# Pooled attention, ELU MoE, SoLU MoE: one pooling moved in the opening, the first pair's PSUM banks and the place of later splits changed in the second MoE

## The chip, the cores and the metric

One core of one Trainium2 chip runs the whole program. The metric is the device time of one execution in microseconds (us), lower is better.

## What is computed

Three stages follow each other on 4608 tokens of 512 features, all in float32:

```
# attention: 8 batches, 8 heads, 576 tokens, head_dim 64, keys and values pooled by 8
k_p = k.reshape(B, H, Sp, 8, D).mean(axis=3);  v_p likewise          # Sp = 72
scores = scale * q @ k_p.T;  attn = softmax(scores);  x = attn @ v_p  # heads joined: (4608, 512)
# first MoE, d_ff 2048
h = x @ w_in;  g = where(h > 0, h, exp(min(h, 0)) - 1);  x = g @ w_out
# second MoE, d_ff 1024
h = x @ w_in2;  solu = h * softmax(h)
ln = (solu - mean(solu)) / sqrt(var(solu) + 1e-6) * g_ln;  out = ln @ w_out2
```

The weights come as 64-bit floats and are turned into 32-bit ones on the chip, by integer operations on their two halves.

## The kernel before, in words

**Precision.** An operand of a large product is split into a high part (a rounded copy, made on ScalarE) and a low part (the difference, made on VectorE or GpSimd); a product is then three matmuls: high by high, low by high, high by low. `xh`, `xl` are the parts of the tokens, `wh`, `wl` of the first weights, `woh`, `wol` of the second, `gh`, `gl_` of the activations.

**Attention.** A unit is one batch and one pair of heads, 32 units in all (`NP` = 4 to a batch). `att_setup(i)` (L122) pools a unit's keys by a reduction on VectorE (L139) and copies the result into a block-diagonal tile; it pools the values on GpSimd (`pool_tree`, L118) for units 0 to 3, and by a reduction on VectorE (L148) for the others. Scores go to PSUM, `att_max` (L176) and `att_exp` take the exponential on ScalarE, `att_soft` (L198) normalises: sum L203, L204, reciprocal L205, product L207. `att_T` transposes on TensorE (L219), `att_V` multiplies by the values, `att_x` (L246) writes `xh` and `xl`.

**The opening.** `startup()` (L689) runs units 0 to 3 and the first weights' conversion (`conv`, L336; `conv_split`, L358) in an order written out by hand, under `tc.manual_schedule()`. All loads are issued from SyncE's queue: keys and queries of units 0 to 3, then values and the first weights (`raw`, L333 for the second weight matrix), then the loads of units 4 and 5 and those after. The keys of all units from 4 on share one buffer (tag `k`, `bufs=1`), so the next load waits until the pooling before has read it. Behind the opening stands `att_setup(NP)` (L773), which is unit 4. Outside of the hand-written part, a scheduling layer sets the order of each engine's instructions, and it may move an instruction ahead of what the code has before it. `with tc.issue_after(x)` puts the block's instructions behind instruction `x` in that order. `gate["soft0"]` is unit 3's L207.

**First MoE.** Nine blocks of 512 tokens by 16 slices of 128 of d_ff. `m_h1` makes 12 matmuls (L461), then comes the ELU (L471 to L492, with `gh` at L485), and `m_o1` makes 12 matmuls (L504) into two PSUM tiles of two banks each, tag A. During block 0 the rest of the weights is converted (L349 to L355) and split (L369, L370); the attention of the following units goes on beside the blocks. `m_out` copies the sums out (L514 on ScalarE, L516 on VectorE) and stores them.

**Second MoE.** 36 tiles of 128 tokens make 18 pairs. `p2_split(n)` (L532) makes the sums and differences of pair n's tokens and their parts (L540 to L550). The two-by-two product of a pair is seven products (`prod`, L558) of six matmuls each (L565), accumulated in three PSUM banks X, Y, Z: in `p2_h_one` B11 to X, B21 to Y, T1 to Z, T2 to X, in `p2_h_two` T3 to X, in `p2_h_three` T4 to X and B22 to Z. Between products into X, ScalarE copies X out (`snap`, L573), and VectorE adds copies to Y and Z (L585, L594, L603), which gives the two rows of sums `ha` and `hb`. `p2_soft` (L609) has a reduction for the maximum (L613), the exponential on ScalarE (L614), the steps to `e` on VectorE (L617 to L621) and the variance (L623 to L625). `p2_T` transposes `e` on TensorE (L635, tag B) and splits it (`dhl`, L638 on ScalarE); `p2_o` makes 24 matmuls (L650, tag C) and stores the result. The eight PSUM banks are split into tag A (2 tiles of two banks), B (2 of one) and C (2 of one). X and Y are the two halves of one tile of tag A; Z is half of the other.

Of the kernel before, what the change touches and what calls it, by code (L numbers as in the profile page):

```python
# [8 lines left out]
F32 = mybir.dt.float32  # L9
# [4 lines left out]
ALU = mybir.AluOpType  # L14
# [4 lines left out]
def kernel(  # L19
# [15 lines left out]
    nc = tc.nc  # L35
# [86 lines left out]
    def att_setup(i, what="kv"):  # L122
        b, p = units[i]
        early = i < NP
        if early:
            k_t, _, v_t = st["kq", p]
            if "kz" not in st:
                kz = sb.tile([P, 4, 512], F32, name="kz", tag="w", bufs=8)
                nc.vector.memset(kz[:, :, 0:2 * SK], 0.0)
                st["kz"] = kz  # L130
            kp = st["kz"][:, p, 0:2 * SK]
            vt = st["kz"][0:SK, p, 2 * SK:2 * SK + P]
        else:
            k_t, v_t = st.pop(("ld", i))
            kp = kpbd[i % 2]
            vt = p1.tile([SK, P], F32, name=f"vt{i}", tag="vt")
        if "k" in what:
            kr = p1.tile([P, SK], F32, name=f"kr{i}", tag="kr", bufs=1)
            nc.vector.tensor_reduce(kr, k_t.rearrange("p (s t) -> p s t", t=POOL), axis=AX, op=ALU.add)  # L139
            cpy = nc.vector.tensor_copy if early else nc.scalar.copy  # L140
            cpy(kp[0:64, 0:SK], kr[0:64, :])
            cpy(kp[64:128, SK:2 * SK], kr[64:128, :])
        if "v" in what:
            vr = p1.tile([SK, P], F32, name=f"vr{i}", tag="vr", bufs=1)
            if early:
                pool_tree(vr, v_t)
            else:
                nc.vector.tensor_reduce(vr, v_t, axis=AX, op=ALU.add)  # L148
            nc.scalar.mul(vt, vr, 1.0 / POOL)
        st["kp", b, p] = (kp, vt)  # L150
# [381 lines left out]
    def p2_split(n):  # L532

        c, q = divmod(n, 2)
        t = wraw["x", c]
        ta, tb = slice(q * P, (q + 1) * P), slice(256 + q * P, 256 + (q + 1) * P)
        sm = sb.tile([P, 4, 2, P], F32, name=f"xs{n}", tag="cv", bufs=2)
        hi, lo = (xtile(f"x{k}{n}").rearrange("p a f -> p (a f)") for k in "hl")
        tt = nc.vector.tensor_tensor
        tt(sm[:, 0], t[:, 0:2, tb], t[:, 2:4, tb], op=ALU.add)  # L540
        tt(sm[:, 1], sm[:, 0], t[:, 0:2, ta], op=ALU.subtract)
        tt(sm[:, 2], t[:, 0:2, ta], t[:, 0:2, tb], op=ALU.subtract)
        tt(sm[:, 3], t[:, 2:4, ta], sm[:, 1], op=ALU.subtract)
        for src, d in ((t[:, :, ta], slice(0, 512)), (t[:, 2:4, tb], slice(512, 768))):
            h, l = (z[:, d].rearrange("p (k t) -> p k t", t=P) for z in (hi, lo))
            nc.scalar.copy(h, src)
            tt(l, src, h.bitcast(F32), op=ALU.subtract)
        src = sm.rearrange("p s k t -> p (s k t)")
        nc.scalar.copy(hi[:, 768:1792], src)
        tt(lo[:, 768:1792], src, hi[:, 768:1792].bitcast(F32), op=ALU.subtract)  # L550
        xc[n] = (hi, lo)
        if q == 1:
            wraw.pop(("x", c))
# [20 lines left out]
        return t  # L574

    def p2_h_one(n):
        xy = ps.tile([P, 2, 512], F32, name="xy", tag="A")
        z = ps.tile([P, 2, 512], F32, name="z", tag="A")
        X, Y, Z = xy[:, 0], xy[:, 1], z[:, 0]
        ha = p2.tile([P, 2, 512], F32, name="ha", tag="h", bufs=3)  # L580
        hb = p2.tile([P, 2, 512], F32, name="hb", tag="h", bufs=3)
        prod(n, X, "A11", "B11", True, False)
        p1s = snap(X)
        prod(n, Y, "A12", "B21", True, True)
        nc.vector.tensor_tensor(ha[:, 0], Y, p1s, op=ALU.add)  # L585
        prod(n, Z, "S1", "T1", True, False)
        prod(n, X, "S2", "T2", False, False)
        acc[n] = (X, Z, ha, hb, snap(X))
# [20 lines left out]
    def p2_soft(i, h):  # L609
        hv = h.rearrange("p a f -> p (a f)")  # L610
        sc = p2.tile([P, 8], F32, name="sc", tag="sc", bufs=6)
        e = p2.tile([P, DFF2], F32, name="e2", tag="e2", bufs=3)
        nc.vector.tensor_reduce(sc[:, 0:1], hv, axis=AX, op=ALU.max, negate=True)  # L613
        nc.scalar.activation(e, hv, AF.Exp, bias=sc[:, 0:1], accum_out=sc[:, 1:2])  # L614
        nc.vector.tensor_scalar(sc[:, 1:2], sc[:, 1:2], 1e-9, None, op0=ALU.add)
        nc.vector.reciprocal(sc[:, 1:2], sc[:, 1:2])
        nc.vector.scalar_tensor_tensor(  # L617
            e, e, sc[:, 1:2], hv, op0=ALU.mult, op1=ALU.mult, accum_out=sc[:, 2:3]
        )
        nc.vector.tensor_scalar(sc[:, 2:3], sc[:, 2:3], 1.0 / DFF2, None, op0=ALU.mult)  # L620
        nc.vector.tensor_scalar(e, e, sc[:, 2:3], None, op0=ALU.subtract)  # L621

        nc.scalar.activation(hv, e, AF.Square, accum_out=sc[:, 3:4])  # L623
        nc.vector.tensor_scalar(sc[:, 3:4], sc[:, 3:4], 1.0 / DFF2, 1e-6, op0=ALU.mult, op1=ALU.add)
        nc.gpsimd.tensor_tensor(sc[:, 4:5], sc[:, 3:4], mhalf, op=ALU.pow)  # L625
        dts[i] = (e, sc)

    def p2_T(i):
        e, sc = dts[i]
        dhl = p2.tile([P, 2, NC2, P], F32R, name="dhl", tag="dhl", bufs=2)  # L630
        dh, dl = dhl[:, 0], dhl[:, 1]
        for g in range(2):
            pt = ps.tile([P, 512], F32, name="pt2", tag="B")
            for c in range(4):
                nc.tensor.transpose(pt[:, c * P:(c + 1) * P], e[:, (4 * g + c) * P:(4 * g + c + 1) * P], ident)  # L635
            d = slice(4 * g, 4 * g + 4)
            dhv = dh[:, d, :].rearrange("p a t -> p (a t)")
            nc.scalar.copy(dhv, pt)  # L638
            nc.vector.tensor_tensor(
                dl[:, d, :].rearrange("p a t -> p (a t)"), pt, dhv.bitcast(F32), op=ALU.subtract  # L640
            )
        dts[i] = (dh, dl, sc)
# [127 lines left out]
    while nload[0] < NP + 2:  # L770
        att_load(nload[0])
        nload[0] += 1
    att_setup(NP)  # L773

    slots = [(j, f) for j in range(NBLK) for f in range(NF)]
    for si, (j, f) in enumerate(slots):
# [64 lines left out]
    def tiles_of(n):  # L841

        c, q = divmod(n, 2)
        return 4 * c + q + 2, 4 * c + q

    for n in range(NPAIR):
        p2_h_one(n)
        if n == 0:
            p2_h_two(n)
            p2_h_three(n)  # L850
            p2_load(1)
            continue
        a, b = tiles_of(n - 1)
        p2_T(a)
        if n % 2 == 0 and n // 2 + 1 < NT // 512:
            p2_load(n // 2 + 1)
        if n >= 2:
            p2_o(tiles_of(n - 2)[1])
        p2_h_two(n)
        if n + 1 < NPAIR:  # L860
            p2_o(a)
        else:
            p2_T(b)
        p2_h_three(n)
        if n + 1 < NPAIR:
            p2_split(n + 1)
            p2_T(b)

    p2_o(a)
# [41 lines left out]
```

## Time and profile before

| | |
|---|---|
| median of 3 timed runs | 1394.13 us (1390.72 to 1394.84) |
| the profiled execution's own time | 1395.61 us |
| its span | 1393.8 us, 16740 instructions |
| TensorE (PE) matmul busy | 1341.8 us (96% of the span) |
| VectorE (DVE) busy | 844.5 us (61%) |
| ScalarE (ACT) busy | 657.1 us (47%) |
| GpSimd (POOL) busy | 306.0 us (22%) |
| chain that ended last, by engine | PE 87%, DVE 6%, DMA 3%, ACT 2% |

Busy time is the time in which an engine had an instruction under way; a busy TensorE need not run at its full clock. PEld is TensorE's loading of weights, which overlaps with PE. SP is SyncE, whose queue (SPq) issues the loads and stores. The chain is followed back from the last instruction, at each step to what released it. The share of an engine over the whole span is a mean of stages with different limits, so the rows further below are read by stage. "L139" is line 139 of the kernel.

### The profile page before, as it was taken

How to read it: one execution, taken by the hardware profiler on the slowest of the kernel's cores; microseconds unless marked ns; L12 is line 12 of the kernel's file. 1: busy time of each engine (PE TensorE's matmuls, PEld its weight loads, DVE VectorE, ACT ScalarE, POOL GpSimd, SP SyncE). 2: the span in 40 equal slices, each digit the busy share in tenths (PEclk: the TensorE clock that was granted, in tenths of full speed). 3: DMA queues.
4: the chain of work that ended last, by engine and by line, in shares of the span. 5: the costliest groups of instructions: out<-in, count | busy, mean ns of one | idle time of the engine just before them, and what ended most of it. 6: DMA issues, size and time to landing. Idle time of an engine off the chain costs nothing.

```text
span 1393.8 us, 16740 instructions
## 1 busy us (share of the span) xinstructions
PE 1341.8 (96%) x6260; PEld 1072.6 (77%) x6260; DVE 844.5 (61%) x1454; ACT 657.1 (47%) x1273; POOL 306.0 (22%) x245
## 2 busy tenths in 40 slices
PE   2889999999999999999999999999899999999998
PEld 2567778788788788788787778887688888888887
DVE  4898766566566566555554375553675666657463
ACT  1677654444444344444444343433455544555453
POOL 2365322222322223222222222221000000000000
PEclk7699999999999999999999999999999999999999
DMA  9255222122022022111010042444211011101000
GB/s 264 71 178 190 78 95 66 33 95 73 27 95 73 28 93 73 35 57 42 27 39 1 17 165 91 151 181 163 86 48 58 24 53 54 54 23 54 29 18 38
DMA packets 48336, 105.93 MB, mean 76 GB/s; under 512 B 4608, under 2 KB 12800, under 8 KB 46848
## 3 DMA queue, kind: packets, MB, share of 16 engines
q1 hardware_dynamic: 48256, 104.88, 22.5%
q8 instruction: 49, 0.80, 0.2%
q14 instruction: 31, 0.25, 0.1%
HBM read 74.45 MB, written 30.41 MB: 75 GB/s over the span
## 4 chain that ended last, share of the span: by engine, by line
PE 87%; DVE 6%; DMA 3%; ACT 2%; issue 1%; SPq 1%; POOL 0%; POOLq 0%; DVEq 0%; ACTq 0%
PE h L461 26%; PE o L504 26%; PE po L650 13%; PE xy L565 9%; PE z L565 3%; PE at L243 2%; PE pt L635 2%; PE at L164 2%; PE pt L219 2%; DMA raw<-in_w 2%; DMA k<-in_k 1%; ACT es L184 1%; DVE cv L353 0%; PE pr L224 0%; DVE cv L355 0%
## 5 line engine op out<-in xcount | busy, mean ns | idle before, releaser
L444 POOL TENSOR_TENSOR wol<-wo,woh 128x512 fp32r<-128x512 f32 x144 | 202.6, 1407 | 524.5 <-ACT woh L443 524.5
L461 PE MATMUL h<-xh,wh 128*128 128x512 f32 x576 | 237.5, 412 | 0.0
L504 PE MATMUL o<-gh,woh 128*128 128x512 f32 x576 | 227.2, 395 | 2.1 <-ACT gh L485 1.6
L461 PE MATMUL h<-xl,wh 128*128 128x512 f32 x576 | 227.7, 395 | 0.0
L504 PE MATMUL o<-gh,wol 128*128 128x512 f32 x576 | 226.5, 393 | 1.0 <-POOL wol L444 1.0
L461 PE MATMUL h<-xh,wl 128*128 128x512 f32 x576 | 226.4, 393 | 0.4 <-POOL wl L370 0.4
L650 PE MATMUL po<-o,dhl 128*128 128x512 f32 x864 | 208.4, 394 | 0.4 <-ACT dhl L638 0.4
L650 PEld LDWEIGHTS po<-o,dhl 128*128 128x128 f32 x864 | 160.9, 188 | 34.7 <-ACT dhl L638 0.7
L482 DVE TENSOR_SCALAR e<-e 128x512 f32<-128x512 f32 x128 | 54.8, 428 | 217.1 <-ACT e L471 216.7
L471 ACT ACTIVATE e<-h 128x512 f32<-128x512 f32 x128 | 76.3, 596 | 198.5 <-PE h L461 198.5
L485 ACT CAST gh<-e 128x512 fp32r<-128x512 f32 x144 | 89.5, 622 | 151.7 <-DVE e L483 141.6
L461 PEld LDWEIGHTS h<-xh,wh 128*128 128x128 f32 x576 | 109.1, 189 | 33.4 <-issue 13.6
L504 PEld LDWEIGHTS o<-gh,woh 128*128 128x128 f32 x576 | 108.4, 188 | 27.8 <-ACT gh L485 3.4
L461 PEld LDWEIGHTS h<-xl,wh 128*128 128x128 f32 x576 | 108.8, 189 | 25.1
L504 PEld LDWEIGHTS o<-gh,wol 128*128 128x128 f32 x576 | 108.5, 188 | 25.1 <-POOL wol L444 1.9
L461 PEld LDWEIGHTS h<-xh,wl 128*128 128x128 f32 x576 | 109.3, 190 | 21.4 <-POOL wl L370 0.9
L625 POOL TENSOR_TENSOR sc<-sc,mhalf 128x1 f32<-128x1 f32 x36 | 22.0, 611 | 385.4 <-DVE sc L620 346.3
L443 ACT CAST woh<-wo 128x512 fp32r<-128x512 f32 x144 | 89.5, 621 | 35.1 <-PE o L504 33.8
L483 DVE TENSOR_TENSOR e<-e,h 128x512 f32<-128x512 f32 x128 | 88.0, 687 | 3.4
L613 DVE TENSOR_REDUCE sc<-hb 128x1 f32<-128x1024 f32 x18 | 22.0, 1220 | 102.3 <-ACT hb L599 101.7
L565 PE MATMUL xy<-T,xh 128*128 128x512 f32 x216 | 77.1, 398 | 3.9 <-DVE sc L620 2.1
L653 ACT ACTIVATE ot<-po,sc 128x512 f32<-128x512 f32 x36 | 24.7, 687 | 106.6 <-PE po L650 88.4
(565 smaller groups left out, 2253.4 us busy)
## 6 DMA issues: line engine op xcount, KB each, us to landing
raw<-in_w SPq DMA_DIRECT2D x48, 512.0 KB
v<-in_v SPq DMA_DIRECT2D x32, 288.0 KB
x1d<-x1s SPq DMA_DIRECT2D x9, 1024.0 KB
x1r<-x1d SPq DMA_DIRECT2D x9, 1024.0 KB
out<-ot SPq DMA_DIRECT2D x36, 256.0 KB
k<-in_k SPq DMA_DIRECT2D x28, 288.0 KB
q<-in_q SPq DMA_DIRECT2D x28, 288.0 KB
w2d<-cv SPq DMA_DIRECT2D x14, 512.0 KB
```

Source lines behind the costliest of these rows:

```text
L164: nc.tensor.matmul(s[:, t * 2 * SK:(t + 1) * 2 * SK], q_t[:, o:o + P], kp, start=True, stop=True)
L219: nc.tensor.transpose(pt[0:SK, t * P:(t + 1) * P], es[:, 2 * t + h, :], ident)
L443: nc.scalar.copy(oh, t[:, f % 4, :])
L444: nc.gpsimd.tensor_tensor(ol, t[:, f % 4, :], oh.bitcast(F32), op=ALU.subtract)
L461: nc.tensor.matmul(h[:, 0:n], a[g][:, kk, fo:fo + P], x[j][:, kk, 0:n], start=(i == 0), stop=(i == 3 * KDM - 1))
L471: nc.scalar.activation(e[:, 0:n], h[:, 0:n], AF.Exp)
L482: nc.vector.tensor_scalar(e[:, 0:n], e[:, 0:n], 1.0, 1.0, op0=ALU.min, op1=ALU.subtract)
L483: nc.vector.tensor_tensor(e[:, 0:n], e[:, 0:n], h[:, 0:n], op=ALU.max)
L485: nc.scalar.copy(gh[:, 0:n], e[:, 0:n])
L504: nc.tensor.matmul(acc, a[:, dm * P:(dm + 1) * P], x[:, 0:n], start=(f == 0 and m == 0), stop=(f == NF - 1 and m == 2))
L565: nc.tensor.matmul(bank, x[:, o:o + P], w[:, y + k, :], start=(start and m == 0), stop=(stop and m == 5), skip_group_check=True,)
L650: nc.tensor.matmul(po, a[:, c, :], w[c // 4][:, c % 4, :], start=(m == 0), stop=(m == 3 * NC2 - 1))
```

## The change

Three edits. The setup of unit 4 is put behind unit 3's normalisation. The first pair of the second MoE takes three single banks from the tags B, B and C in place of two tiles of tag A. The split of pair n+1 (for n from 1) is put behind the last subtraction (L621) of the second softmax that was written before, the one of pair n-1.

```diff
     def p2_h_one(n):
-        xy = ps.tile([P, 2, 512], F32, name="xy", tag="A")
-        z = ps.tile([P, 2, 512], F32, name="z", tag="A")
-        X, Y, Z = xy[:, 0], xy[:, 1], z[:, 0]
+        if n == 0:
+            X, Y, Z = (ps.tile([P, 512], F32, name="xyz", tag=t) for t in "BBC")
+        else:
+            xy = ps.tile([P, 2, 512], F32, name="xy", tag="A")
+            z = ps.tile([P, 2, 512], F32, name="z", tag="A")
+            X, Y, Z = xy[:, 0], xy[:, 1], z[:, 0]
...
-        nc.vector.tensor_scalar(e, e, sc[:, 2:3], None, op0=ALU.subtract)
+        gate["p2"] = nc.vector.tensor_scalar(e, e, sc[:, 2:3], None, op0=ALU.subtract).ins
...
-    att_setup(NP)
+    with tc.issue_after(gate["soft0"]):
+        att_setup(NP)
...
         a, b = tiles_of(n - 1)
+        before = gate["p2"]
         p2_T(a)
...
         if n + 1 < NPAIR:
-            p2_split(n + 1)
+            with tc.issue_after(before):
+                p2_split(n + 1)
             p2_T(b)
```

In the changed file the lines from L577 on have numbers higher by four, those from L778 on by more.

**The opening on VectorE.** In the order of before, the pooling of unit 4's keys (`kr_367` from `k_354`) stands inside unit 0's softmax (`sm_175`, `es_131`), behind its sum:

```order
 L142 COPY kz<-kr_171 64x72
 L203 TENSOR_REDUCE sm_175<-es_131 128x10
-L139 TENSOR_REDUCE kr_367<-k_354 128x72
 L204 TENSOR_SCALAR sm_175<-sm_175 128x10
 L205 RECIPROCAL sm_175<-sm_175 128x10
```

It has left that place. The poolings of units 5 and 6 (`kr_550`, `kr_748`), which stood a few rows further on inside the same opening, have left it too, and stand in the first block of the first MoE now. Unit 4's stands here, behind unit 3's normalisation (`es_209`) and among the first conversions (`cv`):

```order
 L207 TENSOR_TENSOR es_209<-es_209,sm_286 128x720
 L353 SCALAR_TENSOR_TENSOR cv<-raw,cv 128x1024
-L351 TENSOR_SCALAR cv<-cv 128x1024
+L139 TENSOR_REDUCE kr_367<-k_354 128x72
 L355 SCALAR_TENSOR_TENSOR cv<-raw,cv 128x1024
 L257 TENSOR_TENSOR xl_256<-at_291,xh_255 128x512
+L148 TENSOR_REDUCE vr_371<-v_355 72x128
```

The second conversion's first step (L351) went back behind it.

**The passage between the MoEs on TensorE.** `B_7341` is B11, `T_7509` T2, `T_7511` T3; `xh_7707` and `xl_7708` are the parts of pair 0, `xh_7831` those of pair 1, and `o_8_0`, `o_8_1` are the sums of the last block of the first MoE. The last slice of that block:

```order
 L504 MATMUL o_8_1_7230<-gh,wol 128x512
 L504 MATMUL o_8_1_7230<-gl__7775,woh 128x512
+L565 MATMUL xyz<-B_7341,xh_7707 128x512
+L565 MATMUL xyz<-B_7341,xl_7708 128x512
+L565 MATMUL xyz<-B_7341,xh_7707 128x512 x2
+L565 MATMUL xyz<-B_7341,xl_7708 128x512
 L504 MATMUL o_8_0_7229<-gh,woh 128x512
 L504 MATMUL o_8_0_7229<-gh,wol 128x512
 L504 MATMUL o_8_1_7230<-gh,woh 128x512
```

Five of the six matmuls of the first product of the second MoE have come ahead of the last slice's. In the changed order, farther on, between the products T2 and T3 of pair 0:

```order
L565 MATMUL xyz<-T_7509,xh_7707 128x512
L565 MATMUL xy<-B_7341,xh_7831 128x512
L565 MATMUL xy<-B_7341,xl_7832 128x512
L565 MATMUL xy<-B_7341,xh_7831 128x512 x2
L565 MATMUL xyz<-T_7511,xh_7707 128x512
```

Four matmuls of pair 1 stand there now, where before T3's followed T2's at once; four more stand between T3 and T4.

**A later pair on ScalarE.** `e_8760` and `e_8779` are the results of the two exponentials of one pair, `sn` the copy of X in the pair after it, `xh_8972` and `xh_9151` parts made by the splits of two pairs farther on. Before:

```order
L638 CAST dhl<-pt_8804 128x512
L638 CAST dhl<-pt_8811 128x512
L573 COPY sn<-xy 128x512
L614 ACTIVATE e_8779,sc<-ha,sc 128x1024
L549 CAST xh_8972<-xs_8971 128x1024
L546 CAST xh_9151<-x1r_8866 128x512
L546 CAST xh_9151<-x1r_8866 128x256
L623 ACTIVATE hb,sc<-e_8760 128x1024
```

and after (the names' numbers are one higher, the lines four):

```order
L642 CAST dhl<-pt_8805 128x512
L642 CAST dhl<-pt_8812 128x512
L618 ACTIVATE e_8780,sc<-ha,sc 128x1024
L573 COPY sn<-xy 128x512
L627 ACTIVATE hb,sc<-e_8761 128x1024
```

The copy of X stands behind the second exponential, and the casts of the splits, which stood ahead of the squares (L623, now L627), come later.

## Rows read from the trace of the kernel before

**Rows 1.** Stretches: us, length; busy PE, PEld, DVE, ACT, POOL; clock, DMA share, GB/s.

```profile
0.00:58.00 58.00, 25.89 (x113) 17.14 (x114) 35.24 (x62) 19.28 (x41) 14.50 (x24) 0.66 0.66 193
58.00:157.00 99.00, 90.16 (x398) 68.68 (x399) 88.63 (x105) 71.01 (x187) 54.03 (x32) 0.94 0.47 153
157.00:970.00 813.00, 811.46 (x3828) 650.79 (x3827) 463.46 (x759) 353.72 (x672) 215.49 (x155) 1.00 0.22 72
970.00:1005.00 35.00, 29.74 (x120) 22.29 (x119) 20.49 (x43) 13.30 (x23) 1.68 (x2) 0.95 0.38 145
1005.00:1394.00 389.00, 384.57 (x1805) 313.71 (x1803) 236.66 (x488) 199.79 (x352) 20.32 (x34) 1.00 0.11 41
```

**Rows 2.** Waits of VectorE, 0 to 60 us: total us, waits, longest us.

```profile
DVE kr L139 <- DMA k<-in_k: 13.4, 2, 12.7
```

**Rows 3.** Timeline, 0 to 45 us: start, us, what, [idle time before <- releaser].

```profile
12.40 0.20 DVE L142 COPY kz<-kr 64x72 f32<-64x72 f32 x1
...
15.78 1.95 POOL L118 TENSOR_TENSOR v<-v 72x512 f32<-72x512 f32 x2
15.89 1.22 DVE L142 COPY kz<-kr 64x72 f32<-64x72 f32 x1
16.34 4.75 SPq L333 DMA_DIRECT2D raw<-in_w  x2
17.13 0.90 DVE L203 TENSOR_REDUCE sm<-es 128x10 f32<-128x720 f32 x1
...
30.72 0.75 DVE L139 TENSOR_REDUCE kr<-k 128x72 f32<-128x576 f32 x1 [12.68 <-DMA k<-in_k]
...
32.89 1.89 PE L219 MATMUL pt<-ident,es 128*72 128x128 f32 x8 [18.73 <-DVE es L207]
```

**Rows 4.** Timeline, 44 to 75 us: second conversion on ScalarE, TensorE's first `h`.

```profile
46.27 1.12 ACT L349 ACTIVATE wo<-raw 128x1024 f32<-128x1024 f32 x1
...
57.75 0.80 PE L461 MATMUL h<-xh,wh 128*128 128x512 f32 x1
```

**Rows 5.** Timeline of TensorE, 955 to 992 us.

```profile
971.73 0.50 PE L504 MATMUL o<-gh,woh 128*128 128x512 f32 x1 [0.86 <-ACT gh L485]
...
975.24 0.50 PE L565 MATMUL xy<-B,xh 128*128 128x512 f32 x1 [0.50 <-DVE x1s L516]
...
980.13 0.50 PE L565 MATMUL xy<-T,xh 128*128 128x512 f32 x1 [0.42 <-DVE ha L585]
...
982.46 0.50 PE L565 MATMUL xy<-T,xh 128*128 128x512 f32 x1 [0.68 <-ACT sn L573]
...
986.28 0.39 PE L565 MATMUL z<-B,xh 128*128 128x512 f32 x1
```

**Rows 6.** Timeline of TensorE, 990 to 1030 us: the longest idle time.

```profile
994.16 0.51 PE L565 MATMUL xy<-T,xh 128*128 128x512 f32 x1 [2.14 <-DVE sc L620]
```

**Rows 7.** Timeline of VectorE, 950 to 1000 us: splits beside pair 0's softmax.

```profile
988.83 0.68 DVE L547 TENSOR_TENSOR xl<-x1r,xh 128x512 fp32r<-128x512 f32 x1
...
991.03 1.21 DVE L550 TENSOR_TENSOR xl<-xs,xh 128x1024 fp32r<-128x1024 f32 x1
...
994.47 0.75 DVE L621 TENSOR_SCALAR e<-e,sc 128x1024 f32<-128x1024 f32 x1
```

**Rows 8.** Timeline of TensorE, 1094 to 1112 us, in a later pair.

```profile
1101.41 0.39 PE L565 MATMUL z<-T,xl 128*128 128x512 f32 x1
1101.80 0.50 PE L565 MATMUL xy<-B,xh 128*128 128x512 f32 x1
1102.14 0.39 PE L565 MATMUL xy<-B,xl 128*128 128x512 f32 x1
1102.37 0.62 PE L565 MATMUL xy<-B,xh 128*128 128x512 f32 x2
```

**Rows 9.** Timeline of ScalarE, 1085 to 1112 us, in the same pair.

```profile
1101.15 0.60 ACT L573 COPY sn<-xy 128x512 f32<-128x512 f32 x1
1101.63 1.17 ACT L614 ACTIVATE e<-ha,sc 128x1024 f32<-128x1024 f32 x1
```

## The prediction

> **What bounds the kernel now.** I read the busy time by stretches first, then the waits of the opening, then the timelines of the places that the change touches. [rows 1] cut the span into five stretches. From 157 to 970 us TensorE is busy for 811.46 of 813 us, and from 1005 us on for 384.57 of 389: there it is the bound, and nothing that this change does to other engines can shorten its work. What it loses lies in three places: the first 58 us (busy 25.89, and at a mean granted clock of 0.66, so mostly at the lower of its two levels), the first block of the first MoE from 58 to 157 us (8.84 us idle, clock 0.94, VectorE busy for 88.63 of 99 us), and the passage between the two MoEs from 970 to 1005 us (5.26 us idle, clock 0.95). The change works on the first and the last of them; the second decides how much of the first gets through.
>
> **The opening, removed.** [rows 2]: VectorE waits 13.4 us in all, in two waits, for the load of `k` under line 139. The timeline [rows 3] shows the long one. The first softmax's sum (L203) ends at 17.13 + 0.90 = 18.03; the next instruction in VectorE's queue is the pooling of unit 4's keys, whose load lands only at 30.72, 12.68 us later. Unit 0's softmax (L204, L205, L207) stands behind it, and TensorE's transposes behind that: they start at 32.89 after 18.73 us of idleness. The second wait, 13.4 - 12.7 = 0.7 us, is that of unit 5's pooling, somewhat later. The order of the changed kernel puts unit 4's pooling behind unit 3's softmax, and since all later keys use one buffer, units 5 and 6 move still farther back. So 13.4 us of waiting leave VectorE, and two reductions of 0.75 us leave the path up to the first matmul of the MoE, which now starts at 57.75 [rows 4]; I expect it near 57.75 - 13.4 - 1.5 = 42.9.
>
> **What is late next there.** Unit 4's pooling comes up at about 35 us, behind its landing at 30.72. The weights were issued ahead of that load (the last two from 16.34 on, [rows 3]) on the same queue; their second conversion on ScalarE, at 46.27 [rows 4], comes up at about 31.4, so it waits at most a few tenths. On SyncE's queue the load of unit 5's keys waits for unit 4's pooling, with the next weights behind it; those wait for the end of the first conversion anyway, which comes at about the same moment. I cost both at nothing; the cover is some 4 us for the keys, and next to nothing for the weights.
>
> **What the first block keeps of it.** The reductions of units 5 and 6 (1.5 us) are not gone: they now stand in the first block, where VectorE is 90% busy [rows 1]. Bounds: if VectorE sets the pace of this block, only the waiting removed counts, 13.4 us; if TensorE does, 14.9. I take 13.4, because 88.63 of 99 is near to full. The clock can add or take on top: 0.06 of 99 us, 5.9 us, were lost to the lower level here, and the order on TensorE in the block's first third changes, so half of that, 3 us, either way stays in the range.
>
> One thing speaks against. A copy on VectorE that takes 0.20 us (12.40) took 1.22 us at 15.89, while GpSimd pooled values from 15.78 [rows 3]; it ended as GpSimd's first addition did. The new opening runs VectorE's softmax beside such poolings, where the old one stood still. The Trainium skill ("SBUF — State Buffer", section "Who interferes with whom") says that the two share a pair of ports under an exclusive lock, so that the later instruction blocks entirely if it has two SBUF inputs. By that rule two of the four normalisations (L207) could each lose a whole addition, about 1.0 us as the copy did: the opening would give 11.4 and the kernel 1379. By the row alone I add nothing, since the same poolings met the same instructions later in the old order.
>
> **The passage between the MoEs.** [rows 5, 6] list TensorE's idle times: 0.86 us (for ScalarE's `gh`, which stood behind the split of pair 1), 0.50 us (the first product of the second MoE needs a bank of tag A, which VectorE has still to copy out, L516), 0.42 us (the third product waits for `ha`, an addition that reads Y, because X and Y are two halves of one tile), 0.68 us and a like one of 0.67 behind it (each product into X waits for ScalarE's copy of the one before, with nothing to do meanwhile), and 2.14 us at 994.16. Together 5.27 us, and 0.05 of 35 us, 1.75 us, through the clock that follows. In the changed order five matmuls of the first product fill the 0.86 us (five at 0.23, which is the distance from the start of one to the next, 1102.14 to 1102.37 in [rows 8], make 1.15), the second and third wait are void with three separate tiles of tags B, B and C, and four or five matmuls of pair 1 stand between the products that wait for a copy. A copy's wait plus the matmul before it is about 1.1 us, so these are covered just so. The tags B and C are free there: the tile of the slice before last has long been read. The 2.14 us end with VectorE's `ha` of pair 1, in whose queue the splits of pairs 2 and 3 stood between the steps of pair 0's softmax: an L547 of 0.68, an L550 of 1.21 and two shorter ones, some 2.6 us, ahead of the row that finishes `e` at 994.47 + 0.75 = 995.22 [rows 7]. Without them `e` is there at about 992.6 to 993.3. TensorE, which ends the product T4 at 986.28 [rows 5], has 24 matmuls of 0.23 to do before the transposes of that `e`, and comes there at 991.8. So about 1.5 us of waiting are left, for `e` in place of `ha`. The gain is 5.27 - 1.5 = 3.8, and of the clock's 1.75 I count half: 4.6 us. Bounds: all of it, 7.0, or, if `e` is as late as before and the fillers' splits come late, 1.5.
>
> **The later pairs.** From 1005 us on there is nothing to win. What can be lost is in the new order on ScalarE: the copy that frees X (L573), which ran at 1101.15 ahead of the second exponential (1101.63, 1.17 us), now stands behind it [rows 9]. TensorE's next product waits for that copy already now: its first matmul starts 0.39 us after the last one of the product before, not 0.23 (1101.41, 1101.80, [rows 8]), a loss of 0.16 per pair. Behind the exponential the copy ends at about 1101.2 + 1.2 + 0.6 = 1103.0; the order now puts one more matmul of T1 and four of `po` ahead of the waiting one, which would start at 1101.41 + 6 x 0.23 = 1102.8. So the loss is 0.2 to 0.3 per pair instead of 0.16; sixteen pairs make +1 to +2 us. Bounds: -2.5 (the loss goes) and +6 (0.55 per pair, if the exponential is held up by its reduction too). I take +1. The splits themselves have room: a pair's split ends before the pair ahead of it has begun its last products.
>
> **The sum.** -13.4 - 4.6 + 1.0 = -17.0 us. The profiled execution took 1395.61 us, its span being 1393.8; it would take 1378.6. It lies 1.5 us above the median of the timed runs, 1394.13; so I predict a median of **1377 us**.
>
> **Rivals.**
> - *The first block takes part of it back* (1384 us). For it: VectorE is 90% busy there, keys 5 to 8 are loaded later, and each one holds up SyncE's queue with weights behind it. Price: 5 us of the 13.4 and 2 us of the passage. Against it: SyncE's queue already waits for VectorE's conversions there.
> - *The clock stays up* (1368 us): most of the 5.9 us of the first block and all of the passage's 1.75 come back. For it: the passage loses its longest wait. Against it: what brought the clock down in the first block is hardly touched.
> - *The opening was hidden anyway* (1391 us): the weights, not the keys, set the first product. Against it: the second weight load was issued ahead of the keys that landed at 30.72, and the product starts 27 us after that.
> - *Slower* (1401 us): in each of sixteen pairs the copy that frees X, the sum `ha` and the transposes come late one after the other, because exponentials and normalisations now go ahead of them. It decides from 1.3 us per pair on (16 x 1.3 = 21, which is the 17 gained and 0.3% of the time); at 1.5 us per pair the sum is -17 + 24 = +7. For it: three covers of some 0.2 us each. Against it: the moved split instructions leave room in the same queue.
>
> **How the numbers follow.** About 0.3% (4.2 us) is what a measurement of this kernel can tell from no change. Chances: forecast 0.70 (1371 to 1382 by itself), first block 0.14, clock 0.07, hidden 0.05, slower 0.04. Faster: 0.70 + 0.14 + 0.07 = 0.91; same 0.05; slower 0.04. The range 1370 to 1386 holds the forecast's bounds, half of the clock's case and two thirds of the first block's.
>
> **What would show it.** Right: no wait of VectorE over 1 us for a `k` load in the opening, the first `h` matmul at 42 to 45 us, the first block ending at 142 to 145 us, TensorE's idle time between the MoEs under 2.5 us with the longest wait before the transposes of pair 0, and the period of a later pair within 0.3 us of the present. Wrong: a first `h` matmul that starts early and a first block that ends less than 10 us earlier (first block); a wait for weights before 45 us (hidden); a period per pair over 1 us longer, with TensorE waiting for L573 (slower).

## The result, and the profile after

| | before | after |
|---|---|---|
| median of the timed runs | 1394.13 us (1389.33 to 1394.99, 5 runs) | 1376.76 us (1375.50 to 1379.65, 5 runs) |
| ratio | | 0.9883, 95% interval 0.9867 to 0.9899 |
| profiled execution, span | 1395.61, 1393.8 us | 1376.92, 1375.1 us |

The change makes the kernel 17.4 us faster by the medians. Run again beside the experiments below, it took 1377.02 us against 1393.13, a ratio of 0.9888 (0.9873 to 0.9902). The forecast of 1377 holds. Two of the terms behind it do not: by the means of the profiles below, the opening and the first block brought 2.7 us less than the sum had, the second MoE 2.2 us more.

The page of the changed kernel, busy time and the shares of the chain by engine:

```profile
PE 1335.4 (97%) x6260; PEld 1067.3 (78%) x6260; DVE 853.5 (62%) x1454; ACT 657.3 (48%) x1273; POOL 304.0 (22%) x245
...
PE 86%; DVE 5%; DMA 4%; ACT 3%; issue 2%; SPq 0%; POOL 0%; POOLq 0%; DVEq 0%; ACTq 0%
```

VectorE executes as many instructions as before and is busy for 9 us more, about half of it in the first block of the first MoE (101.58 to 106.26 us, below). That is the first hint of what the sum missed.

To compare the two traces I cut them at the same four instructions: the first `h` matmul (L461), the first copy of the sums of the first block, block 0 (L514), the last `h` matmul, and the last scaled output (L653, after the change L657). For before, the stretches between the first two, from the last `h` to the first output, and from there to the last output (columns as in [rows 1]):

```profile
57.75:180.70 122.95, 114.11 (x516) 87.85 (x515) 101.58 (x124) 82.26 (x210) 60.61 (x36) 0.95 0.41 133
967.70:1005.30 37.60, 32.34 (x132) 24.41 (x131) 22.56 (x46) 13.91 (x25) 1.68 (x2) 0.95 0.38 140
1005.30:1390.30 385.00, 384.27 (x1804) 313.48 (x1802) 236.66 (x488) 199.11 (x352) 20.32 (x34) 1.00 0.11 41
```

and after:

```profile
42.14:168.80 126.66, 113.04 (x515) 86.52 (x514) 106.26 (x127) 83.53 (x215) 58.65 (x37) 0.97 0.42 134
955.90:987.10 31.20, 29.71 (x132) 23.25 (x131) 20.02 (x38) 13.93 (x25) 1.47 (x2) 1.00 0.46 169
987.10:1371.60 384.50, 383.88 (x1804) 312.36 (x1802) 243.07 (x497) 199.49 (x352) 20.55 (x34) 1.00 0.11 41
```

The first `h` matmul comes 15.6 us earlier, the first block takes 3.7 us longer, the passage is 6.4 us shorter, the later pairs 0.5 us; the stretch between block 0 and the passage is 0.1 us longer. -15.6 + 3.7 - 6.4 - 0.5 + 0.1 = -18.7, which is the difference of the spans.

**The opening.** Waits of VectorE in the first 60 us (total, count, longest), the two largest:

```profile
DVE kr L139 <- DMA kq<-in_k: 4.5, 2, 2.9
DVE mx L180 <- PE at L164: 1.5, 1, 1.5
```

The 13.4 us of [rows 2] are gone. What stands first now is the load of the first keys (`kq`), which was there before as well. The timeline of all engines (start, us; in brackets the idle time before):

```profile
14.10 2.00 POOL L118 TENSOR_TENSOR v<-v 72x512 f32<-72x512 f32 x2 [12.47 <-DMA v<-in_v]
14.44 0.98 DVE L141 COPY kz<-kr 64x72 f32<-64x72 f32 x1
...
16.56 1.95 POOL L118 TENSOR_TENSOR v<-v 72x512 f32<-72x512 f32 x2
16.59 1.25 DVE L204 TENSOR_SCALAR sm<-sm 128x10 f32<-128x10 f32 x1
...
19.42 1.89 PE L219 MATMUL pt<-ident,es 128*72 128x128 f32 x8 [6.24 <-DVE es L207]
...
32.40 1.15 ACT L349 ACTIVATE wo<-raw 128x1024 f32<-128x1024 f32 x1 [0.39 <-DMA raw<-in_w]
...
34.27 0.75 DVE L139 TENSOR_REDUCE kr<-k 128x72 f32<-128x576 f32 x1
...
42.14 0.80 PE L461 MATMUL h<-xh,wh 128*128 128x512 f32 x1
...
43.42 1.17 ACT L349 ACTIVATE cv<-raw 128x1024 f32<-128x1024 f32 x1 [2.29 <-DMA raw<-in_w]
```

The transposes of unit 0 start at 19.42, in [rows 3] at 32.89. Unit 4's pooling, at 34.27, waits for nothing, as forecast at "about 35 us". `h` starts at 42.14, forecast 42.9. The prediction's sign for the rival "hidden", a wait for weights before 45 us, is there: ScalarE waits 2.29 us for them at 43.42. But the first `h` had started by then, so the weights did not set it.

**The passage.** TensorE's timeline; only two rows have an idle time:

```profile
958.85 0.39 PE L565 MATMUL xyz<-B,xh 128*128 128x512 f32 x1
...
976.39 0.50 PE L565 MATMUL xy<-T,xh 128*128 128x512 f32 x1 [0.82 <-DVE ha L589]
...
978.72 0.50 PE L565 MATMUL xy<-T,xh 128*128 128x512 f32 x1 [0.68 <-ACT sn L573]
979.05 0.40 PE L565 MATMUL xy<-T,xl 128*128 128x512 f32 x1
979.29 1.03 PE L639 MATMUL pt<-ident,e 128*128 128x128 f32 x8
```

Of the 5.27 us of [rows 5, 6], 1.50 are left, and they belong to pair 1, which still has X and Y in one tile of tag A. The transposes at 979.29 wait for nothing.

### The profile page after: what moved, and what is told of

Its sections match the earlier page's. It is cut to its first block, busy times and chain, and to the rows that moved or that the text cites. A ratio compares the mean times of both kernels' runs of the same rounds, so it can differ in the third digit from the quotient of the medians.

```text
span 1375.1 us, 16753 instructions
## 1 busy us (share of the span) xinstructions
PE 1335.4 (97%) x6260; PEld 1067.3 (78%) x6260; DVE 853.5 (62%) x1454; ACT 657.3 (48%) x1273; POOL 304.0 (22%) x245
## 4 chain that ended last, share of the span: by engine, by line
PE 86%; DVE 5%; DMA 4%; ACT 3%; issue 2%; SPq 0%; POOL 0%; POOLq 0%; DVEq 0%; ACTq 0%
PE h L461 25%; PE o L504 25%; PE po L654 14%; PE xy L565 9%; PE z L565 3%; DMA raw<-in_w 3%; PE at L243 2%; PE at L164 2%; PE pt L639 2%; PE pt L219 2%; ACT es L184 1%; DMA w2d<-cv 1%; PE xyz L565 1%; DVE cv L353 0%; DVE cv L355 0%
## 5 line engine op out<-in xcount | busy, mean ns | idle before, releaser
L461 PE MATMUL h<-xh,wh 128*128 128x512 f32 x576 | 237.0, 411 | 1.1 <-DVE e L478 1.1
L461 PE MATMUL h<-xl,wh 128*128 128x512 f32 x576 | 227.4, 395 | 0.0
L461 PE MATMUL h<-xh,wl 128*128 128x512 f32 x576 | 225.5, 392 | 0.0
L654 PE MATMUL po<-o,dhl 128*128 128x512 f32 x864 | 213.5, 394 | 0.4 <-ACT dhl L642 0.4
L461 PEld LDWEIGHTS h<-xh,wh 128*128 128x128 f32 x576 | 108.6, 189 | 34.6 <-issue 13.6
L461 PEld LDWEIGHTS h<-xl,wh 128*128 128x128 f32 x576 | 108.5, 188 | 25.1
L461 PEld LDWEIGHTS h<-xh,wl 128*128 128x128 f32 x576 | 108.9, 189 | 20.3
L565 PE MATMUL xy<-T,xh 128*128 128x512 f32 x204 | 71.7, 392 | 1.5 <-DVE ha L589 0.8
L657 ACT ACTIVATE ot<-po,sc 128x512 f32<-128x512 f32 x36 | 24.8, 688 | 90.1 <-PE po L654 50.0
```

Of the source, the lines that this page charges most:

```text
L461: nc.tensor.matmul(h[:, 0:n], a[g][:, kk, fo:fo + P], x[j][:, kk, 0:n], start=(i == 0), stop=(i == 3 * KDM - 1))
L565: nc.tensor.matmul(bank, x[:, o:o + P], w[:, y + k, :], start=(start and m == 0), stop=(stop and m == 5), skip_group_check=True,)
L654: nc.tensor.matmul(po, a[:, c, :], w[c // 4][:, c % 4, :], start=(m == 0), stop=(m == 3 * NC2 - 1))
```

## The experiments

For each kernel the traces give four moments and three differences (us): first `h` matmul, from there to the first copy of block 0's sums ("block 0"), from there to the last group of `h` ("steady"; the group starts 0.45 us ahead of the last `h` matmul), and from there to the last output ("second MoE").

| kernel | median | first h | block 0 | steady | second MoE |
|---|---|---|---|---|---|
| before | 1394.13 | 57.8 | 122.9 | 786.6 | 423.0 |
| opening alone | 1383.06 | 40.4 | 127.3 | 788.1 | 421.9 |
| banks alone | 1387.87 | 55.2 | 122.3 | 786.9 | 417.6 |
| splits alone | 1391.05 | 57.0 | 122.1 | 785.2 | 420.8 |
| banks and splits | 1388.18 | 55.7 | 122.3 | 787.0 | 417.1 |
| after | 1376.76 | 42.1 | 126.7 | 786.6 | 416.2 |
| after, again | 1377.02 | 40.2 | 127.6 | 786.6 | 416.4 |
| before, light | 1390.62 | 56.0 | 120.4 | 786.6 | 422.0 |
| after, light | 1371.86 | 40.3 | 123.0 | 785.1 | 416.6 |
| after, no trees | 1376.01 | 39.7 | 127.6 | 785.4 | 416.2 |
| after, copies on ScalarE | 1376.35 | 39.5 | 127.0 | 788.8 | 416.3 |
| after, no splits | 1377.74 | 40.2 | 128.1 | 785.4 | 417.7 |

Five kernels with the old opening start `h` at 55.2 to 57.8 (mean 56.3). The five that have the new one, with nothing else changed ahead of it, start at 40.2 to 42.1 (mean 40.6). That is 15.7 us, and it shows that one profile places this moment to a microsecond or two only: before's own profile had the latest of the old starts.

**The opening alone.** Before, with

```diff
-    att_setup(NP)
+    with tc.issue_after(gate["soft0"]):
+        att_setup(NP)
```

> Unit 4's setup behind unit 3's normalisation, the second MoE as before. Theory A (the three edits work in places that do not touch and add up): the first h matmul at 42.1 us and the end of the first block 11.9 us earlier, as in the changed kernel; time 12 us under before, ratio 0.9915. Rival B (the opening's gain shrinks once the passage between the MoEs is unchanged, or the other way round): 8 us or less, or 14 us and more. From the passage on the trace should be that of before, shifted: 5.3 us of TensorE idle time there.

Measured: 1383.06 us against 1392.31 for before beside it, ratio 0.9927 (0.9912 to 0.9942), so some 9 to 10 us. `h` starts at 40.4, block 0 takes 127.3. The start is earlier than theory A has it, the time lies between its 12 us and rival B's 8: the 17.4 us by which `h` starts earlier than in before's profile have shrunk to 13.0 at the first copy of block 0's sums (11.1 against the mean of the four kernels with the old opening and the poolings unchanged). The passage is that of before, shifted, as expected: 5.6 us of waits, the longest 2.2.

**Banks alone, splits alone, both.** The second edit of the diff in the kernel before; the third edit; both.

> Only the three single PSUM banks for the first pair of the second MoE. Theory A (banks and splits each end waits of their own): the idle times of 0.86, 0.50, 0.42, 0.68 and 0.67 us go, the one of 2.14 us stays, with the low clock behind it: 3.1 us less idle, time 3 to 4 us under before, ratio 0.9975. Rival B (the 2.14 us only take the gain: VectorE's queue decides when e is there, so TensorE just waits longer): the longest wait grows to about 5 us and the time is that of before. Rival C (the banks bring all of the passage): 6.4 us under before.

> Only the splits of later pairs behind the softmax. Theory A: the idle time of 2.14 us shrinks to 1.5 or less, the five shorter ones stay; 0.6 to 2.1 us, with the clock 0.6 to 4 us under before; the later pairs within 1 us of before (385.0 us from the first output to the last), though ScalarE's copy of X now stands behind the second exponential. Rival B (that copy costs 0.3 us in each of sixteen pairs): the later pairs 5 us longer, the time 3 us over before.

> Banks and splits, the opening as before. Theory A: the passage 6.4 us shorter as in the changed kernel (1.5 us of idle time left, clock 1.00), the later pairs 0.5 us shorter, the time 7 us under before, ratio 0.995; and what the two give alone adds up to it. Rival B: they need each other, so that the sum of the two alone is 3 us or less, or either alone gives it all.

Measured against 1392.31: banks 0.9967 (0.9955 to 0.9980), splits 0.9989 (0.9977 to 1.0000), both 0.9967 (0.9955 to 0.9980). In the traces the second MoE loses 4.3 to 5.4 us by the banks (417.6 against the 421.9 to 423.0 of the three kernels that lack both edits), 1.1 to 2.2 by the splits, 4.8 to 5.9 by both. So they overlap: the splits add about half a microsecond to the banks. TensorE's timeline of banks alone shows it:

```profile
985.24 0.50 PE L565 MATMUL xy<-T,xh 128*128 128x512 f32 x1 [0.69 <-DVE ha L589]
...
988.11 0.50 PE L565 MATMUL xy<-T,xh 128*128 128x512 f32 x1 [1.21 <-ACT sn L573]
...
990.43 0.50 PE L565 MATMUL xy<-T,xh 128*128 128x512 f32 x1 [0.68 <-ACT sn L573]
...
991.23 1.03 PE L639 MATMUL pt<-ident,e 128*128 128x128 f32 x8
```

The 2.14 us of [rows 6] have gone without the splits' edit. Neither theory A nor rival B or C of the banks has that. In splits alone the same wait shrank to 0.5 us (TensorE's waits, 955 to 1006 us; total, count, longest):

```profile
PE xy L565 <- ACT sn L573: 1.3, 2, 0.7
PE o L504 <- ACT gh L485: 0.9, 1, 0.9
PE xy L565 <- DVE sc L620: 0.5, 1, 0.5
```

Either edit removes most of it, so the second of them finds little.

**The changed kernel again, and without its third edit.**

> The changed kernel once more, beside the kernels below on one chip. The opening alone gave a ratio of 0.9927, banks and splits together 0.9967. Theory A (the two places add up): 0.9927 times 0.9967 is 0.9894, some 14.7 us under before. Rival B (the parts help each other): 0.988 or less, 16.7 us or more. On the trace, theory A: first h matmul at 40 to 43 us, 126 to 128 us from there to the copy of the first block's sums, 31 to 32 us from the last h matmul to the first output.

```diff
-            with tc.issue_after(before):
-                p2_split(n + 1)
+            p2_split(n + 1)
```

> The changed kernel without its third edit: the splits of later pairs where they were. The kernel with banks alone took 1387.87 us, that with banks and splits 1388.18. Theory A (with the banks in place the splits' new order is worth nothing): the same time as the changed kernel, 1377 within 2 us, the passage with 2.6 us of TensorE idle time in place of 1.5 and the later pairs giving that back. Rival B (the prediction's: without it TensorE waits 2 us more for e): 1379 us or more.

Measured: the changed kernel 0.9888 (0.9873 to 0.9902) of before, where 0.9927 times 0.9967 is 0.9894. The two places add up (theory A), and rival B's 0.988 lies within the interval but is not needed. Without the splits' edit: 1377.74 us, 0.9880 (0.9864 to 0.9897) of its own runs of before. That cannot be told from the changed kernel. Its trace has TensorE waits of 1.9 us for `sn` and 0.7 for `ha` in the passage, the 2.6 us of theory A, and a second MoE of 417.7 us, not 416.2 or 416.4.

**Who sets the pace of block 0.** In both kernels the poolings of units 7 to 10, which stand in block 0, were made light: they copy a part of the keys and values in place of summing them, and so leave out work of VectorE.

```diff
+            if 7 <= i <= 10:
+                nc.vector.tensor_copy(kr, k_t[:, 0:SK])
+            else:
                 nc.vector.tensor_reduce(kr, k_t.rearrange("p (s t) -> p s t", t=POOL), axis=AX, op=ALU.add)
...
+                if 7 <= i <= 10:
+                    nc.vector.tensor_copy(vr, v_t[:, :, 0])
+                else:
                     nc.vector.tensor_reduce(vr, v_t, axis=AX, op=ALU.add)
```

> The changed kernel, with VectorE's pooling of keys and values left out for units 7 to 10, which stand in the first block: instead of summing eight entries it copies the first of eight values, and the first 72 of 576 keys. That takes some 4 x 1.55 = 6.2 us of work from VectorE there. Theory A (VectorE sets the pace of the first block): the 126.7 us from the first h matmul to the copy of the block's sums shrink by 4 to 6 us. Rival B (TensorE and its clock set it): by 1 us or less.

> The same work left out (pooling of units 7 to 10) in the kernel before. Theory A (VectorE sets the pace there as well): the 122.9 us from the first h matmul to the copy of the first block's sums shrink by 4 to 6 us. Rival B (before, VectorE had room in this block, and only the two poolings that came in from the opening used it up): by 1 to 2 us here, and by more in the changed kernel.

Block 0 in the changed kernel, its profile of the second time (columns as in [rows 1]):

```profile
40.20:167.80 127.60, 114.45 (x516) 87.39 (x514) 108.22 (x127) 83.66 (x215) 56.64 (x37) 0.95 0.41 133
```

in the kernel with banks and splits, whose opening is the old one:

```profile
55.70:178.00 122.30, 112.19 (x515) 86.14 (x514) 103.05 (x124) 82.34 (x210) 61.33 (x36) 0.97 0.41 134
```

in the changed kernel with light poolings:

```profile
40.30:163.30 123.00, 112.23 (x516) 86.16 (x515) 102.82 (x127) 83.37 (x215) 58.23 (x37) 0.97 0.43 138
```

and in the kernel before with light poolings:

```profile
56.00:176.40 120.40, 111.16 (x515) 85.18 (x514) 98.81 (x124) 81.64 (x209) 60.53 (x36) 0.98 0.41 136
```

In the changed kernel VectorE is busy for 5.4 us less and the block is 4.6 shorter (3.7 to 5.1 against the four profiles with the new opening: opening alone, after, after again, no splits); the time went from 1377.02 to 1371.86. So VectorE's work is on the path there, as theory A has it. It is not all of these 4.6 us: TensorE's idle time, the length less its busy time, fell by 2.4 (13.15 to 10.77), and its busy time by 2.2, beside a granted clock of 0.97 in place of 0.95. The first profile of the changed kernel has 0.97 with full poolings; against that one the block is 3.7 shorter, of which 2.9 are idle time. Whether the lighter work brought the clock up in the other 2.2 us was not tried.

In the kernel before the block got 2.0 us shorter (122.4 is the mean of the four old ones: before, banks, splits, both) and the time 2.5 (1393.13 to 1390.62). By the block that is rival B, 1 to 2 us here and more in the changed kernel. And here the idle time of TensorE did not clearly fall: 9.24 us, against 8.84 in before and 10.11 in the kernel with banks and splits. What got shorter is mostly its busy time, beside a clock of 0.98 against 0.95 and 0.97. So VectorE's pace is shown for the changed kernel, and not for the kernel before.

**Where VectorE's time went up.** VectorE's groups in block 0 (line, operation, count, busy us, mean ns), in the kernel with banks and splits, whose opening is the old one:

```profile
L355 DVE SCALAR_TENSOR_TENSOR cv<-raw,cv 128x1024 uint32<-128x1024 uint32 x6 | 8.7, 1450 | 0.1
...
L353 DVE SCALAR_TENSOR_TENSOR wo<-raw,wo 128x1024 uint32<-128x1024 uint32 x8 | 11.2, 1402 | 0.1
...
L139 DVE TENSOR_REDUCE kr<-k 128x72 f32<-128x576 f32 x5 | 3.7, 739 | 0.0
...
L492 DVE TENSOR_TENSOR gl__800<-e,gh 128x512 fp32r<-128x512 f32 x1 | 0.7, 678 | 0.0
```

and in the changed kernel, the second profile:

```profile
L353 DVE SCALAR_TENSOR_TENSOR wo<-raw,wo 128x1024 uint32<-128x1024 uint32 x8 | 13.4, 1671 | 0.0
...
L355 DVE SCALAR_TENSOR_TENSOR cv<-raw,cv 128x1024 uint32<-128x1024 uint32 x7 | 10.5, 1503 | 0.0
...
L139 DVE TENSOR_REDUCE kr<-k 128x72 f32<-128x576 f32 x7 | 5.2, 741 | 0.0
...
L492 DVE TENSOR_TENSOR gl__800<-e,gh 128x512 fp32r<-128x512 f32 x1 | 1.8, 1781 | 0.0
```

VectorE is busy for 5.2 us more (103.05 to 108.22). Two poolings moved in, 1.5 us. One more last step of a conversion (L355) falls behind the first `h` now, about 1.2. The other 2.5 are a balance of instructions of the same shape. The eight L353 of `wo` take 2.2 us more, and five of sixteen L492 take 1.6 to 1.9 us instead of three, at 0.7 for the others; against that the seven L351 of `wo` take 1.7 us less and the eight small L182 2.3 less. GpSimd itself is busy for 4.7 us less there (61.33 to 56.64).

The trace of the changed kernel, second profile, shows what the long ones have in common (GpSimd, then VectorE):

```profile
81.31 1.37 POOL L370 TENSOR_TENSOR wl<-cv,wh 128x512 fp32r<-128x512 f32 x1 [2.79 <-ACT wh L369]
```

```profile
81.45 1.78 DVE L492 TENSOR_TENSOR gl__673<-e,gh 128x512 fp32r<-128x512 f32 x1
```

All five long L492 start while an instruction of GpSimd is running and end 0.55 us after it, as this one does (82.68 and 83.23); the eleven short ones start with none running. So they waited for GpSimd, as the opening's steps do (next experiment). What the block would take without that was not tried.

**What TensorE waits for in block 0.** The releasers of its idle time show that VectorE is not alone. By the means of the four profiles with the old opening and of the four with the new one, waits ended by VectorE rose from 4.4 to 5.5 us, those ended by ScalarE from 4.0 to 6.8, and those ended by GpSimd fell from 1.5 to 0.8. The longest one in the changed kernel's second profile (ScalarE, then TensorE):

```profile
75.00 1.12 ACT L349 ACTIVATE wo<-raw 128x1024 f32<-128x1024 f32 x1 [3.88 <-DMA raw<-in_w]
```

```profile
79.05 0.63 PE L219 MATMUL pt<-ident,es 128*72 128x128 f32 x4 [2.51 <-ACT es L184]
```

ScalarE stood still for weights, and the exponentials that TensorE waited for came behind that. Its longest wait for weights in block 0 is 1.5 to 1.8 us in the four old profiles and 2.8 to 3.9 in the four new ones; with light poolings it is still 3.3. SyncE issued these weights at 67.53, as VectorE's last step of the conversion before them (L355) ended at 67.45, and next behind a load of keys that had waited for a pooling until 66.32. No run moved those loads, so what made the weights late is open.

**GpSimd's additions beside the opening's softmax.** The changed kernel, with GpSimd's pooling of units 0 to 3 cut to its last addition:

```diff
-                pool_tree(vr, v_t)
+                nc.gpsimd.tensor_tensor(vr, v_t[:, :, 0], v_t[:, :, 1], op=ALU.add)
```

> The changed kernel, with most of GpSimd's pooling of the values of units 0 to 3 left out: only the last of its additions is done, on the first two of eight entries. Theory A (VectorE's small steps at 14.44, 16.59, 18.13, 22.13 and 23.53 us waited for GpSimd's additions, 3.3 us in all, and that is on the path): these steps take 0.19, 0.17, 0.91, 0.17 and 0.91 us, and the first h matmul comes 2 to 3.3 us earlier, near 39. Rival B (they waited, but something else, such as loads or TensorE, sets the opening's end): the same short steps, the first h matmul within 1 us of 42. Rival C (they did not wait for GpSimd): the steps stay as long as they are.

VectorE's timeline there:

```profile
14.59 0.19 DVE L141 COPY kz<-kr 64x72 f32<-64x72 f32 x1
...
15.96 0.17 DVE L204 TENSOR_SCALAR sm<-sm 128x10 f32<-128x10 f32 x1
...
16.41 0.91 DVE L207 TENSOR_TENSOR es<-es,sm 128x720 f32<-128x720 f32 x1
```

All five steps have their short time, so rival C falls: they did wait for GpSimd. `h` starts at 39.7, 2.4 us earlier than in the profile in which they were long, but only 0.5 us earlier than in the second profile of the changed kernel. That second profile tells theory A from rival B (GpSimd, then VectorE):

```profile
12.21 1.95 POOL L118 TENSOR_TENSOR v<-v 72x512 f32<-72x512 f32 x2 [10.59 <-DMA v<-in_v]
```

```profile
14.73 1.22 DVE L142 COPY kz<-kr 64x72 f32<-64x72 f32 x1
...
16.91 0.19 DVE L204 TENSOR_SCALAR sm<-sm 128x10 f32<-128x10 f32 x1
```

Here the values landed 1.9 us earlier (12.21, not 14.10), GpSimd was done sooner, and only one copy was held up for long. VectorE's order is the same in both profiles, and the second normalisation (L207) ends at 22.52 here, at 24.66 there. The other three profiles with this opening have 0.5 to 0.9 us of such delays and start `h` at 40.2 to 40.4. The same program meets the collision or misses it, by when a load lands, and this is worth up to 2 us of its opening. The time, 1376.01 against 1377.02, does not tell the two apart.

**Copies on ScalarE.** The changed kernel, with

```diff
-            cpy = nc.vector.tensor_copy if early else nc.scalar.copy
+            cpy = nc.scalar.copy
```

> The changed kernel, with the copies of the pooled keys of units 0 to 3 (lines 141 and 142, eight of 0.19 to 1.2 us) on ScalarE in place of VectorE. Theory A (VectorE's queue sets the end of the opening): the first h matmul 1 to 2 us earlier than the 40.2 to 42.1 us of the changed kernel, and the time 1 to 2 us under 1377, which is within what can be told from no change. Rival B (loads set it): first h matmul at 40 to 42 us as before, the time the same. Rival C (the longer way through ScalarE comes late for TensorE's scores): first h matmul 1 us later or more.

Measured: `h` at 39.5, 1376.35 us, 0.9869 (0.9854 to 0.9884) of its runs of before. That is 1.1 us earlier than the mean of 40.6, as theory A has it, but inside the spread of that moment, and the time is the same within what can be told. It is not a version that is shown to beat the change.

## Why the prediction was right, and which of its terms were not

**The opening, right.** -13.4 for the waits and -1.5 for two poolings make -14.9 up to the first `h`; measured -15.6 between the two profiles and -15.7 between the means. The sign "at 42 to 45 us" held in the first profile alone; the others start `h` at 39.5 to 40.4. That weights and the next loads cost nothing up to there held too: in the changed kernel's profile ScalarE waits 0.39 us for the weights at 32.40, against "at most a few tenths".

**What the first block keeps of it, the step that was mis-sized.** The prediction took back 1.5 us, for the two poolings that moved in, and gave their reason: VectorE at 90% of this block. Measured, block 0 took 5.0 us longer (127.4, the mean of four, against 122.4). Of these, 3.3 are idle time of TensorE (9.8 to 13.1) and 1.7 its busy time, beside a lower clock, which the prediction had left to its range (3 us either way) and not to its sum. The reading that VectorE's work counts there holds for the changed kernel. But the term counted only two instructions that move in, and neither the waits for GpSimd nor those of TensorE for ScalarE, which grew most, by 2.8 us. So the net of the opening was -10.7 where the sum had -13.4.

The first rival had just this price, 5 us of the 13.4, and a chance of 0.14. Its mechanism, keys that hold up SyncE's queue with weights behind them, is neither shown nor excluded: a lighter VectorE brings 4.6 us back, yet the wait for weights that grew stands right ahead of the exponentials that TensorE waits for longest. How the 5.0 us divide among these causes stays open.

**GpSimd beside VectorE.** The opening's steps beside GpSimd were held up, as the copy in [rows 3] was: 0.98 us for 0.19, 1.25 for 0.17. The prediction weighed this with the Trainium skill ("SBUF — State Buffer", section "Who interferes with whom"), which gives VectorE and GpSimd one pair of ports under an exclusive lock; the traces agree. By that rule, as the prediction applied it, two normalisations (L207) would lose 1.0 us each. Measured, L207 took 1.14 us for 0.91, and small steps ahead of it lost the time instead. In the first profile this comes to 3.3 us (0.98 - 0.19 for L141, 1.25 and 1.11 less 0.17 each for L204, twice 0.23 for L207), in the second to about 1. "By the row alone I add nothing" was too little there: the first profile starts `h` at 42.1, the second at 40.2. It did not show against the forecast of 42.9, which both beat.

**The passage, the mechanism right, the size low.** All five short waits of [rows 5] went as said. The 2.14 us were to leave 1.5 for `e`; they left none, and 1.50 stayed elsewhere, in pair 1's own products. The idle time left is the forecast one, but at another place. VectorE's rows, the first from before, the others from after, show why `e` is not late:

```profile
984.84 0.69 DVE L594 TENSOR_TENSOR hb<-z,sn 128x512 f32<-128x512 f32 x1 [2.09 <-ACT sn L573]
```

```profile
970.34 0.69 DVE L598 TENSOR_TENSOR hb<-xyz,sn 128x512 f32<-128x512 f32 x1 [4.96 <-ACT sn L573]
...
977.96 0.75 DVE L625 TENSOR_SCALAR e<-e,sc 128x1024 f32<-128x1024 f32 x1
```

Counted from the last `h` matmul (967.73, then 955.87), pair 0's sum `hb` comes at 14.5 us in place of 17.1, since TensorE no longer waits ahead of it. The prediction moved `e` up by the splits alone, to 24.9 to 25.6 us; it is ready at 22.8, and the transposes start at 23.4.

The gain was 6.4 against 4.6, because of what the sum counted at half or not at all: TensorE was busy for 29.71 us there, not 32.34, for the same 132 matmuls. About 1.7 of that is the clock of before's profile, 0.50 from 994.7 to 998.1 us, where the changed kernel has 1.00 all through. In the kernel with the opening alone, waits about as long as before's, 5.6 us in all, left the clock at 1.00 too, and so did the kernel before with light poolings, so that low stretch is not a cost of the waits to be counted on; without it the second MoE gains 5.4 (421.9 to 416.5, the mean of the kernels with both edits), later pairs included. Part of the rest is that a matmul after a wait takes 0.50 us and the next starts 0.33 later (the rows at 978.72 and 979.05 above), where they take 0.39 and start 0.23 apart otherwise: a wait cost about 0.1 us more than its idle time here.

**The splits, wrong as a term of their own.** The prediction put the end of the 2.14 us down to them. With the banks in place they are worth 0.5 to 1.5 us in the traces, and nothing that the times show. With the banks alone the transposes do not wait for `e` either (991.23 above): TensorE has products of pair 1 to do before them, with the 2.6 us of waits shown there.

**The later pairs, right.** +1 us with bounds of -2.5 and +6; measured -0.5. The copy that frees X does stand behind the second exponential now. In a pair of the changed kernel, ScalarE and then TensorE:

```profile
1082.80 1.16 ACT L618 ACTIVATE e<-ha,sc 128x1024 f32<-128x1024 f32 x1
...
1083.94 0.58 ACT L573 COPY sn<-xy 128x512 f32<-128x512 f32 x1
```

```profile
1083.50 1.08 PE L654 MATMUL po<-o,dhl 128*128 128x512 f32 x4
1084.58 0.50 PE L565 MATMUL xy<-B,xh 128*128 128x512 f32 x1
```

The copy ends at 1084.52 and the product starts at 1084.58. The four `po` matmuls end their turn at 1083.50 + 4 x 0.23 = 1084.42, so the wait is about 0.16 us, as it was. The rival "slower" needed 1.3 us per pair.

**The sum.** -15.7 + 5.0 for opening and block, -5.8 for the second MoE (422.3 to 416.5, means of the three kernels with neither and of the six with both edits), nothing for the steady stretch (786.5 and 786.6 in the mean): -16.5, against -17.0 forecast and 16.1 and 17.4 measured. That the number is right to 0.3 us is owed to two misses of opposite sign, +2.7 and -2.2. That is luck, and so is that before's profile, against which the sum was made, has a late opening and a low clock in the passage. The price of the rival "clock", 1368, does not come out of its own terms: 5.9 us and the other half of 1.75 from 1377 make 1370.

## What to carry to other kernels

When a wait goes away ahead of a stretch in which another engine is near to full, count that engine's work in the stretch anew, with what it does more slowly beside its neighbours, and not only the instructions that move in. When an edit removes waits of the engine that feeds a chain, move the whole chain up by them. When two edits aim at one wait, cost each with the other in place. And a term of one or two microseconds out of a single profile (a late load, a stretch at a lower clock) is to be looked for in a second execution before it is booked as a gain.

## What the runs showed of the hardware

The same program started its first `h` matmul at 42.1 us in one execution and at 40.2 in another, because a load that landed at 14.1 or at 12.2 us brought GpSimd's additions beside VectorE's small steps, or did not. A `tensor_scalar` of 128x10 then took 1.25 us in place of 0.17. In block 0 a `tensor_tensor` of 128x512 that started while GpSimd was at work on two tensors of that size ended 0.55 us after GpSimd's did, and took 1.78 us in place of 0.68. TensorE's granted clock fell to a mean of 0.69 from 995 to 1000 us, behind the waits of the passage, in before's profile, and stayed at 1.00 in two other kernels' profiles with waits about as long. In block 0 its mean was 0.95 in one execution of the changed kernel and 0.97 in another.
